# Weighted values of a block computed in two halves around one second-layer slice

## The chip, the cores and the metric

The kernel runs on one NeuronCore of a Trainium2 chip. The metric is the device time of one execution in microseconds (us), lower is better; the time before is the median of three runs. One further execution was taken with the hardware profiler, and every line shown below is of that execution. PE is TensorE (its weight loads are shown apart, as PEld), DVE is VectorE, ACT is ScalarE, POOL is GpSimd, SP is SyncE, which issues most DMAs.

## The reference

Attention with a banded mask and eight global keys, then a two-layer network on its output:

```python
scores = scale * np.matmul(q, k.transpose(0, 1, 3, 2)) + bias      # 4 batches, 8 heads, 768 rows, 64 columns
scores = np.where(keep, scores, -1e9)                               # the last 96 keys and the first 8
a = exp(scores - max); a = a / (sum(a) + 1e-9)
x = (a @ v)                                                         # 3072 rows of 512
h = x @ w_in                                                        # 512 -> 2048
out = (h * np.clip(h + 3.0, 0.0, 6.0) / 6.0) @ w_out                # 2048 -> 512
```

## The kernel before

The 3072 rows are worked on in 8 blocks of 384 rows (two for each batch, numbered 0 to 7). For each block the kernel makes the attention output x, then runs the two layers over 16 slices f of the 2048 hidden columns. `first` (L172) is the first layer of a slice: 12 matmuls of 128x384 into one PSUM bank named hp, of which there are two. `gate`, `high` and `rest` (ACT, DVE, POOL, DVE) turn hp into the pair gh and gl. `second` (L204) is the second layer of a slice: 9 matmuls of 128x512 into the three acc banks. The operands of both layers are in a float32 form that PE takes in one pass, so each such matmul leaves two PE records, one weight load and one matmul.

From block 2 on (`twos`, L490), slices go in twos: the first layer of two slices (L495), then `finish` of the two slices before (L500-501), and so on. Between these come `yield`s; at the k-th of them the caller runs the list `units[k]`, which holds the attention work of the next block (`attention`, L709). So while block i is in its layers, the attention of block i+1 is strewn between them. One round of `twos` has four yields, so k = 24 and 25 come after the first layers of slices 12 and 13, and k = 26 comes after the second layers of slices 10 and 11, just ahead of the first layers of slices 14 and 15.

Attention of a block, for each of four pairs of heads: `packed` makes the scores, then come softmax (DVE, ACT, POOL), a 32x32 transpose on DVE into the tile blocks (L948, `spread`) and four DMAs into the tile weights (`send`). The last pair's `send` is in units[21]. In units[26] stands `weighted` (L686): the products of weights with values for all four pairs. It walks over chunks of 32 keys, first the chunk of the global keys (384 wide) and then those of the band (32 to 128 wide). For each chunk it issues 8 matmuls, two for each pair, each on a 32x64 part of the PE array, and each pair adds up in a bank of its own: sp, tp, xp and one of the two hp banks. These operands are plain float32, which PE takes in two passes; each such matmul leaves four PE records. Blocks 3, 5 and 7 have 16 chunks (128 matmuls), blocks 4 and 6 have 13 (104 matmuls). After the last chunk `put_x` copies each bank to xh (ACT, L158) and xl (DVE, L159), which also frees the hp bank for slice 15, and a DMA fetches the next block's values (L309).

The order of PE, SP and POOL instructions is pinned to the program order (`in_order`, L663). DVE and ACT are ordered by a scheduler. Blocks 0 and 1 and the attention of block 2 (`rest_of_third`, L673) are worked on by other loops; `rest_of_third` calls `weighted` too.

## Time and profile before

| What | Value |
|---|---|
| median of 3 runs | 653.87 us (652.95 to 654.45) |
| the profiled execution | 655.53 us |
| its span, first to last instruction | 653.7 us |
| its mean granted PE clock | 0.995 of full speed |
| DVE, ACT, POOL busy | 54%, 39%, 25% of the span |
| HBM | 73 GB/s over the span |

The page gives busy time by engine, the chain of work that ended last, and groups of instructions. A timeline row has the start, the duration, engine, line, operation, the tile written and those read, the shape, a count, and in square brackets the idle time of the engine ahead of it with what ended it. "issue" there means that the engine waited for nothing that the profile shows. [...]

### The profile page before, as it was taken

How to read it: one execution, taken by the hardware profiler on the slowest of the kernel's cores; microseconds unless marked ns; L12 is line 12 of the kernel's file. 1: busy time of each engine (PE TensorE's matmuls, PEld its weight loads, DVE VectorE, ACT ScalarE, POOL GpSimd, SP SyncE). 2: the span in 40 equal slices, each digit the busy share in tenths (PEclk: the TensorE clock that was granted, in tenths of full speed). 3: DMA queues.
4: the chain of work that ended last, by engine and by line, in shares of the span. 5: the costliest groups of instructions: out<-in, count | busy, mean ns of one | idle time of the engine just before them, and what ended most of it. 6: DMA issues, size and time to landing. Idle time of an engine off the chain costs nothing.

```text
span 653.7 us, 14423 instructions
## 1 busy us (share of the span) xinstructions
PE 634.9 (97%) x5593; PEld 560.6 (86%) x5593; DVE 354.8 (54%) x1066; ACT 255.3 (39%) x706; POOL 166.5 (25%) x371
## 2 busy tenths in 40 slices
PE   8989999999999999999989999899999999999997
PEld 7778899888888888888978889888887888899985
DVE  5889999995645552356424554245523555222222
ACT  6897777775424321332223241143212522121111
POOL 5667000001423330134302332023310242012100
PEclk9999999999999999999989999899999999999999
DMA  7575454434423422233212241123311311110001
GB/s 281 181 239 173 138 159 156 141 120 142 117 60 116 117 59 44 81 108 81 67 67 77 59 117 31 67 78 82 93 31 66 102 38 31 33 40 10 1 1 54
DMA packets 34334, 59.78 MB, mean 91 GB/s; under 512 B 3280, under 2 KB 21200, under 8 KB 33488
## 3 DMA queue, kind: packets, MB, share of 16 engines
q1 hardware_dynamic: 33968, 58.50, 30.2%
q8 instruction: 46, 0.75, 0.5%
q14 instruction: 32, 0.26, 0.1%
q10 hardware_dynamic: 288, 0.26, 0.1%
HBM read 41.16 MB, written 6.29 MB: 73 GB/s over the span
## 4 chain that ended last, share of the span: by engine, by line
PE 88%; DVE 5%; ACT 2%; issue 2%; POOL 2%; DMA 1%; POOLq 0%; ACTq 0%
PE hp L172 40%; PE acc L204 35%; PE sp L873 2%; PE sp L204 2%; PE xp L204 1%; PE tp L204 1%; DVE xl L159 1%; ACT n L906 1%; POOL n L926 1%; PE sp L702 1%; DVE n L902 1%; PE tp L702 1%; PE xp L702 1%; DMA iv<-bounds 1%; PE tp L873 1%
## 5 line engine op out<-in xcount | busy, mean ns | idle before, releaser
L183 ACT ACTIVATE g<-hp,small 128x384 f32<-128x384 f32 x127 | 73.6, 580 | 264.3 <-PE hp L172 172.8
L172 PE MATMUL hp<-xh,w1h 128*128 128x384 f32 x512 | 175.2, 342 | 0.5 <-DVE xl L159 0.4
L172 PE MATMUL hp<-xh,w1l 128*128 128x384 f32 x512 | 173.9, 340 | 0.1
L172 PE MATMUL hp<-xl,w1h 128*128 128x384 f32 x512 | 173.1, 338 | 0.0
L190 POOL TENSOR_SCALAR gh<-g 128x384 fp32r<-128x384 f32 x104 | 53.3, 513 | 433.8 <-DVE g L184 405.0
L184 DVE SCALAR_TENSOR_TENSOR g<-g,hp 128x384 f32<-128x384 f32 x128 | 70.7, 553 | 125.4 <-ACT g L183 124.5
L204 PE MATMUL acc<-w2h,gh 128*128 128x512 f32 x336 | 132.7, 395 | 0.0
L204 PE MATMUL acc<-w2h,gl 128*128 128x512 f32 x336 | 131.8, 392 | 0.0
L204 PE MATMUL acc<-w2l,gh 128*128 128x512 f32 x336 | 131.7, 392 | 0.0
L197 DVE TENSOR_TENSOR gl<-g,gh 128x384 fp32r<-128x384 f32 x128 | 71.4, 558 | 66.1 <-POOL gh L190 60.3
L172 PEld LDWEIGHTS hp<-xh,w1h 128*128 128x128 f32 x512 | 97.3, 190 | 6.1 <-issue 1.9
L906 ACT ACTIVATE n<-n,least 128x136 f32<-128x136 f32 (+2 forms) x192 | 79.6, 416 | 53.6 <-DVE least L902 52.8
L172 PEld LDWEIGHTS hp<-xl,w1h 128*128 128x128 f32 x512 | 97.1, 190 | 2.6
L172 PEld LDWEIGHTS hp<-xh,w1l 128*128 128x128 f32 x512 | 97.0, 190 | 0.9 <-DVE w1l L439 0.8
L926 POOL TENSOR_SCALAR n<-n,sums 128x136 f32<-128x136 f32 (+2 forms) x186 | 81.8, 456 | 39.2 <-DVE sums L917 23.8
L204 PEld LDWEIGHTS acc<-w2h,gh 128*128 128x128 f32 x336 | 63.1, 188 | 14.7 <-issue 3.0
L204 PEld LDWEIGHTS acc<-w2h,gl 128*128 128x128 f32 x336 | 63.1, 188 | 13.7 <-DVE gl L197 0.3
L204 PEld LDWEIGHTS acc<-w2l,gh 128*128 128x128 f32 x336 | 63.1, 188 | 11.5
L948 DVE STREAM_TRANSPOSE blocks<-n 128x256 f32<-128x256 f32 x138 | 51.0, 423 | 22.6 <-POOL n L926 21.2
L906 ACT ACTIVATION_READ_ACCUMULATOR n<-n,least 128x1 f32 x192 | 36.0, 187 | 0.0
L399 ACT ACTIVATE wz<-wst 128x512 f32<-128x512 f32 x32 | 21.5, 676 | 5.9 <-DVE w2l L439 3.8
L446 DVE CUSTOM_DVE_ANT_0 wz<-wz,we 128x1024 uint16<-128x1024 uint16 x32 | 22.2, 695 | 1.2 <-POOL we L404 0.9
(126 smaller groups left out, 722.9 us busy)
## 6 DMA issues: line engine op xcount, KB each, us to landing
wst<-w SPq DMA_DIRECT2D x32, 512.0 KB, 3.6
load<-pairs SPq DMA_DIRECT2D x31, 444.0 KB, 3.5
weights<-blocks SPq DMA_DIRECT2D x92, 120.0 KB, 2.4
values<-values SPq DMA_DIRECT2D x6, 1024.0 KB, 5.0
out<-o SPq DMA_DIRECT2D x23, 256.0 KB, 2.3
values<-pairs SPq DMA_DIRECT2D x9, 384.0 KB, 3.4
out<-o ACTq DMA_DIRECT2D x1, 256.0 KB, 2.8
load<-pairs SPq DMA_DIRECT2D x1, 252.0 KB, 4.0
```

What stands on the lines that cost most here:

```text
L172: self.nc.tensor.matmul(hp, lhsT=self.w1(w, f)[:, kt, :], rhs=a[:, kt, :], start=(n == 0), stop=(n == 3 * NKT - 1))
L183: nc.scalar.activation(out=g, in_=hp, func=AF.Relu, bias=self.three, scale=1.0)
L184: nc.vector.scalar_tensor_tensor(out=g, in0=g, scalar=6.0, in1=hp, op0=ALU.min, op1=ALU.mult)
L190: self.nc.gpsimd.tensor_scalar(out=gh, in0=g, scalar1=1.0, scalar2=0.0, op0=ALU.mult, op1=ALU.add)
L197: self.nc.vector.tensor_tensor(out=gl, in0=g, in1=gh.bitcast(F32), op=ALU.subtract)
L204: self.nc.tensor.matmul(acc[tt], lhsT=a[:, tk], rhs=self.w2(w, f), start=(f == 0 and j == 0), stop=(f == NF - 1 and j == 2))
L399: self.nc.scalar.activation(out=self.z[i].bitcast(F32), in_=words[:, :, 1].bitcast(F32), func=AF.Abs)
L446: tt(out=z, in0=z, in1=self.e.pop(i), op=ALU.add)
L702: nc.tensor.matmul(out[pr][j * D:(j + 1) * D, g0 * GQ:g1 * GQ], lhsT=self.values_of[own, c, j * D:(j + 1) * D], rhs=groups[own, j, g0:g1, ...
L906: nc.scalar.activation(out=e[:, j, lo:end], in_=e[:, j, lo:end], func=AF.Exp, bias=self.least[:, i:i + 1], scale=-1.0, accum_out=self.sums ...
L926: nc.gpsimd.tensor_scalar(out=e[:, j, lo:end], in0=e[:, j, lo:end], scalar1=over, scalar2=0.0, op0=ALU.mult, op1=ALU.add)
L948: nc.vector.transpose(out=self.blocks[:, :, t, 4 * s:4 * s + 4], in_=e[:, :, c:c + P].rearrange("p j (b q) -> p j b q", b=4))
```

## The change

`weighted` becomes a generator that yields once, ahead of chunk number len(chunks) // 2. At k = 25 the caller puts its first half into a list, `between`; `twos` runs what is in that list after the second layer of the first of the two pending slices. The second half, with `put_x` and the DMA for the next values, stays at k = 26. For blocks 3 to 7 the order on PE is then: second layer of slice 10, first half of the products, second layer of slice 11, second half. The four banks hold partial sums over the second layer of slice 11. In `rest_of_third` the generator is run through at once, so the products of block 2 stay in one piece.

```diff
@@ twos
             for self.last in self.pending:
                 self.finish()
+                if self.between:
+                    self.between.pop()()
@@ banded
-        self.pending = []
+        self.pending, self.between = [], []
@@ rest_of_third
-        units[2 * slices - 1].append(lambda: self.weighted(pairs[:-1]))
+        units[2 * slices - 1].append(lambda: list(self.weighted(pairs[:-1])))
@@ weighted
-        for c, g0, g1, slot in chunks:
+        for n, (c, g0, g1, slot) in enumerate(chunks):
+            if n == len(chunks) // 2:
+                yield
@@ attention
-        units[26].append(lambda: self.weighted(pairs[:NPAIR]))
+        values = self.weighted(pairs[:NPAIR])
+        units[25].append(lambda: self.between.append(lambda: next(values)))
+        units[26].append(lambda: next(values, None))
```

PE's order before, for block 3: the last three matmuls of slice 11's second layer, then the products, whose chunk of the global keys (64x384 as the program counts the two halves of a row) comes first.

```order
L204 MATMUL acc<-w2h_1030,gh 128x512
L204 MATMUL acc<-w2l_1031,gh 128x512
L204 MATMUL acc<-w2h_1030,gl 128x512
L702 MATMUL sp<-weights,values 64x384 x2
L702 MATMUL tp<-weights,values 64x384 x2
L702 MATMUL xp<-weights,values 64x384 x2
L702 MATMUL hp<-weights,values 64x384 x2
L702 MATMUL sp<-weights,values 64x32 x2
```

All 64 rows of products follow one another there. Now the same place on PE with the change (L702 has become L706): what stands ahead of the eighth chunk's end and behind it.

```order
L706 MATMUL tp<-weights,values 64x128 x2
L706 MATMUL xp<-weights,values 64x128 x2
L706 MATMUL hp<-weights,values 64x128 x2
L204 MATMUL acc<-w2h_1030,gh 128x512
L204 MATMUL acc<-w2l_1031,gh 128x512
L204 MATMUL acc<-w2h_1030,gl 128x512
```

The nine L204 matmuls of slice 11, which stood ahead of the first product, now stand behind the 64th matmul of 128; the first half has moved nine matmuls forward, and the second half and everything after it stand where they stood. On DVE, ACT, POOL and SP nothing changes its order on the path that runs.

## The prediction

> **What bounds the kernel now.** The page first: how busy the engines are, the instruction queue, and who is on the chain that ended last.

> ```profile
> span 653.7 us, 14423 instructions
> PE 634.9 (97%) x5593; PEld 560.6 (86%) x5593; DVE 354.8 (54%) x1066; ACT 255.3 (39%) x706; POOL 166.5 (25%) x371
> ...
> q8 instruction: 46, 0.75, 0.5%
> ...
> PE 88%; DVE 5%; ACT 2%; issue 2%; POOL 2%; DMA 1%; POOLq 0%; ACTq 0%
> ...
> weights<-blocks SPq DMA_DIRECT2D x92, 120.0 KB, 2.4
> ```

> PE is the bound: 97% busy and 88% of the chain. A reorder on PE pays only if it removes time in which PE does nothing or runs slowly. Two per cent of the chain is "issue", so the second view is PE's timeline. These rows are, by time, the entry into block 3's products, the two rows around each stop inside the products of blocks 3 to 7, one row each of blocks 3 and 4 used below, and the rows where the first layer of slices 14 and 15 begins and where the second layer after it begins.

> ```profile
> 253.66 0.39 PE L204 MATMUL acc<-w2h,gl 128*128 128x512 f32 x1
> 253.98 0.54 PE L702 MATMUL sp<-weights,values 32*64 32x384 f32 x2
> ...
> 255.50 0.28 PE L702 MATMUL tp<-weights,values 32*64 32x128 f32 x2
> ...
> 257.25 0.24 PE L702 MATMUL sp<-weights,values 32*64 32x96 f32 x1
> 258.62 0.29 PE L702 MATMUL sp<-weights,values 32*64 32x96 f32 x1 [1.11 <-issue]
> ...
> 332.01 0.28 PE L702 MATMUL xp<-weights,values 32*64 32x128 f32 x2
> ...
> 333.73 0.24 PE L702 MATMUL xp<-weights,values 32*64 32x64 f32 x2
> 335.86 0.27 PE L702 MATMUL hp<-weights,values 32*64 32x64 f32 x2 [1.89 <-issue]
> ...
> 336.21 0.44 PE L172 MATMUL hp<-xh,w1h 128*128 128x384 f32 x1
> ...
> 342.04 0.39 PE L204 MATMUL acc<-w2h,gh 128*128 128x512 f32 x1
> ...
> 412.08 0.27 PE L702 MATMUL tp<-weights,values 32*64 32x96 f32 x2
> 414.10 0.30 PE L702 MATMUL xp<-weights,values 32*64 32x96 f32 x2 [1.76 <-issue]
> ...
> 414.77 0.45 PE L172 MATMUL hp<-xh,w1h 128*128 128x384 f32 x1
> ...
> 420.62 0.39 PE L204 MATMUL acc<-w2h,gh 128*128 128x512 f32 x1
> ...
> 490.41 0.22 PE L702 MATMUL hp<-weights,values 32*64 32x64 f32 x1
> 492.05 0.18 PE L702 MATMUL sp<-weights,values 32*64 32x32 f32 x1 [1.43 <-issue]
> ...
> 492.17 0.22 PE L702 MATMUL hp<-weights,values 32*64 32x32 f32 x2
> 492.32 0.44 PE L172 MATMUL hp<-xh,w1h 128*128 128x384 f32 x1
> 492.61 0.34 PE L172 MATMUL hp<-xl,w1h 128*128 128x384 f32 x1
> ...
> 497.07 0.39 PE L204 MATMUL acc<-w2h,gh 128*128 128x512 f32 x1
> ...
> 567.15 0.26 PE L702 MATMUL xp<-weights,values 32*64 32x96 f32 x2
> 568.61 0.30 PE L702 MATMUL hp<-weights,values 32*64 32x96 f32 x2 [1.19 <-issue]
> ```

> Each of the five blocks stops once inside its products, late, with no engine or data transfer named as the cause. From start to start the stops last 1.37, 2.13, 2.02, 1.64 and 1.46 us, 8.62 in all. Where do they come? The view of busy time by stretches, for L702 alone, counts the passes ahead of each stop (x behind the PE figure):

> ```profile
> 253.90:257.60 3.70, 3.53 (x211) 3.03 (x211) 1.00 0.01 4
> 330.60:334.20 3.60, 3.27 (x189) 2.87 (x190) 1.00 0.02 5
> 408.70:412.60 3.90, 3.61 (x216) 3.13 (x216) 1.00 0.02 4
> 487.30:490.90 3.60, 3.31 (x194) 2.90 (x195) 1.00 0.02 5
> 563.70:567.60 3.90, 3.66 (x221) 3.18 (x221) 1.00 0.01 4
> ```

> A pass is two records, so the stops come 422, 378, 432, 388 and 442 records into the products. A block's program has on PE 16 first layers of 24 records, 16 second layers of 18, four packed score groups of 96, and the products: 1568 records with 128 product matmuls, 1472 with 104. From stop to stop that makes 1568-422+378 = 1524, then 1526, 1524, 1526. The DMA view has the instruction queue's packets in between; these rows are the stretches from 256.2 to 333.6 us and from 333.5 to 333.6.

> ```profile
> q8 instruction: 6, 0.10, 0.5%
> ...
> q8 instruction: 1, 0.02, 59.1%
> ```

> Six packets between two stops (the three stretches after are alike), so one packet holds 1525/6 = 254 records. **Every stop is at a packet's edge, the second edge inside the same products.** My reading: PE's instructions arrive in packets, the next is fetched when an edge is passed, and it takes longer than PE needs for a packet of tiny matmuls. The edge before block 4's stop lies 127 passes earlier, at pass 62, about 332.0 us. From there the 127 passes run until 333.73, or 1.72 us; the packet moves at 333.5 and PE goes on at 335.86. So passing an edge to going on takes 3.85 us in the longest case (3.12 in block 3, by the same count from about 255.5).

> [...]

> A second loss follows the two longest stops. The view by stretches, now for all engines, from the first matmul after the products:

> ```profile
> 336.20:339.00 2.80, 2.80 (x14) 2.80 (x11) 1.95 (x4) 1.63 (x4) 0.00 (x0) 0.57 0.52 152
> 414.80:417.00 2.20, 2.20 (x11) 2.20 (x9) 1.76 (x4) 1.55 (x4) 0.00 (x0) 0.57 0.48 104
> ```

> The granted clock is 0.57 there. The two first layers take 342.04-336.21 = 5.83 and 420.62-414.77 = 5.85 us, against 497.07-492.32 = 4.75 in block 6, whose stop of 1.64 was followed by no dip. The dips cost 1.08 + 1.10 = 2.18 us.

> **The change part by part.** *Where the edges fall now.* The first half starts 18 records (one slice) earlier in the program, and what stands ahead of it is the same, so the edges keep their record numbers. The first edge falls 186, 142, 196, 152 and 206 records into the first half (stop minus 254 plus 18). That half holds 8 chunks or 256 records, 6 chunks or 192 in blocks 4 and 6. So in all five blocks the first edge is inside the first half, with 40 records to spare at least, and the second edge is inside the second half. The slice lies between them.

> *What the slice buys.* The chain of waits has 18 second-layer matmuls in one row:

> ```profile
> 559.71 4.12 PE acc L204 x18
> ```

> so nine take 2.06 us. Between the edges there are now 118 passes (1.60 us at 1.72 per 127), the slice (2.06) and one more change between array shapes each way (0.34, below): 4.00 us, where 1.72 stood. The longest need was 3.85. All five stops should end, by 0.15 us in block 4 and by more elsewhere: minus 8.62, plus 0.07 for five normal distances, is **minus 8.55**. A need 0.5 us longer than measured would leave some 0.35 in block 4, 0.3 in block 5, and nothing in block 3.

> *The dips.* Without the stops PE is idle for no stretch near 1.7 us there, and I take them as gone: **minus 2.18**. [...]

> *What is added.* One more way out of the products into full matmuls and one more way in, per block. Way in: 253.98-253.66 = 0.32 instead of 0.23 between starts, 0.09. Way out: from the last pass (492.17) to 492.32, and 0.29 instead of 0.17 to the next, together 0.25. That is 0.34 per block, **plus 1.7** for five. The trace has no way out to L204 in these blocks; the bounds are 0.09 a block (the weight loads hide) and 0.6 (twice the way out and the way in), 0.5 to 3.0 in all. I take 0.34, which is what both rows show.

> *What costs nothing, and why.* The first half starts 2.06 us earlier, in block 4 at 328.63 instead of 330.69. It needs the last weights: DVE's transposes and the bank of slice 12 are done early, as DVE's timeline has it:

> ```profile
> 321.81 0.77 DVE L948 STREAM_TRANSPOSE blocks<-n 128x256 f32<-128x256 f32 x2 [0.56 <-POOL n L926]
> ...
> 325.21 0.56 DVE L184 SCALAR_TENSOR_TENSOR g<-g,hp 128x384 f32<-128x384 f32 x1 [2.63 <-ACT g L183]
> ```

> The transposes end at 322.58 and the DMAs behind them land 2.4 us after issue by the page's median, so near 325, with 3.6 us to spare. The hp bank is free when slice 12's gate has read it, at 325.77, 2.9 us ahead. Gone cover would cost PE the lateness itself, once a block. Holding the banks costs nothing: sp, tp and xp are next asked for by the score groups of the next block, and the second hp bank by slice 15, after `put_x` as before. No DMA and no POOL or SP instruction moves. `put_x` stays behind the second half, so slice 15 waits for its bank as it does now; that is in the 4.75.

> Sum on the profiled execution: 655.53 - 8.55 - 2.18 + 1.7 = 646.5. That execution was 1.66 us over the median of the runs, about what one to two dips are worth, so the runs may hold fewer dips. Taking one from the median: 653.87 - 8.55 - 1.09 + 1.7 = **645.9**.

> **The rivals.** *The stop moves along (other side).* If the stop is set off by reaching the second edge at speed, not by time since the first, it keeps its length in the second half, and the change only adds 1.7: 655.6. It decides on when the fetch starts: at the first edge or at the end of what is there. Against it: in block 4 the packet moves at 333.5, before PE stops at 333.73. [...] 7%.

> *The fetch takes longer* than 4.0 us, because its start hangs on how far ahead PE reads and not on what PE executes: the longer stops keep up to 1 us each, and one dip may stay. About 649. For it: only 0.15 us to spare in block 4. 9%.

> *The dips stay*, from the low array use of the products: 653.87 - 8.55 + 1.7 = 647.0. Against it: blocks 3, 6 and 7 have the same products and no dip. 8%.

> *The split does nothing measurable*, savings and switches cancelling, near 653.5: 4%.

> **How the numbers follow.** The forecast holds 72%, with 643.5 (both dips in the runs, switches at 0.5) to 648.5 (switches at 3.0, small rests of the stops). The range 643.0 to 650.0 takes in the longer fetch and the staying dips and leaves out the other two, 11%, and some of the tails. A measurement of this kernel can tell about 0.2%, 1.3 us, from no change: faster 0.89, same 0.05, slower 0.06.

> **What would show it.** Right: no "issue" idle inside L706 in blocks 3 to 7, instruction packets still six to a block and the first edge in the first half, granted clock 1.0 in the first layers that follow, and L204 between two runs of L706 with starts of about 0.3 us at both joints. Wrong: an "issue" idle of over 1 us in a second half (the stop moves), the clock at 0.57 without one (the dips), joints far over 0.34 us, or PE waiting for DMA or DVE ahead of the first half.

## The result, and the profile after

The changed kernel takes 647.76 us (median of 4 runs, 647.15 to 648.35), against 654.16 (652.95 to 655.25, 4 runs): a ratio of 0.9903, 95% interval 0.9882 to 0.9923. The profiled execution took 647.65 us with a span of 645.9, against 655.53 and 653.7. The page of the changed kernel:

```profile
span 645.9 us, 14423 instructions
PE 634.3 (98%) x5593; PEld 557.5 (86%) x5593; DVE 354.9 (55%) x1066; ACT 255.9 (40%) x706; POOL 167.4 (26%) x371
```

The same instructions take 7.8 us less. PE's idle time fell by 7.2 us, from 18.8 to 11.6. Its busy time is hardly changed (634.9 us before, 634.3 now), because two things nearly cancel in it: the stretches of slow clock (2.25 us) went, and the joints (the changes between the products and full matmuls, 2.4 us, both below) came. The view of waits of PE (what waited, for what; us, times, longest) shows the idle time that is left:

```profile
PE xp L972 <- DVE xl L159: 1.9, 3, 1.1
PE xp L972 <- issue: 1.4, 1, 1.4
PE tp L940 <- ACT pt L944: 1.0, 1, 1.0
PE xp L386 <- DVE small L108: 0.9, 1, 0.9
PE sp L897 <- DMA load<-pairs: 0.6, 1, 0.6
PE hp L172 <- DVE xl L159: 0.3, 2, 0.2
```

No wait of L706, the products, is left in any of the five blocks, for "issue" or for a transfer. The 1.4 us of "issue" at L972 belongs to the first stage and stands in the trace before as well (1.42 us ahead of 44.26). PE's timeline around blocks 3 and 4 has the joints and the first layers that follow:

```profile
252.24 0.40 PE L204 MATMUL acc<-w2h,gl 128*128 128x512 f32 x1
252.57 0.54 PE L706 MATMUL sp<-weights,values 32*64 32x384 f32 x2
...
254.70 0.28 PE L706 MATMUL hp<-weights,values 32*64 32x128 f32 x2
254.91 0.50 PE L204 MATMUL acc<-w2h,gh 128*128 128x512 f32 x1
255.25 0.39 PE L204 MATMUL acc<-w2l,gh 128*128 128x512 f32 x1
...
256.86 0.39 PE L204 MATMUL acc<-w2h,gl 128*128 128x512 f32 x1
257.18 0.32 PE L706 MATMUL sp<-weights,values 32*64 32x128 f32 x2
...
326.19 0.39 PE L204 MATMUL acc<-w2h,gh 128*128 128x512 f32 x1
...
334.26 0.45 PE L172 MATMUL hp<-xh,w1h 128*128 128x384 f32 x1
...
338.97 0.39 PE L204 MATMUL acc<-w2h,gh 128*128 128x512 f32 x1
```

The second half follows the slice at the distance of the first entry, 0.32 us; the way out of the first half takes 0.21 and then 0.34 instead of 0.23. These are distances from start to start: the rows overlap, as L204 has a duration of 0.39 us where the next starts 0.23 later. Behind block 4 the two first layers take 338.97 - 334.26 = 4.71 us, where 5.83 stood, and the clock, in the view by stretches from 334.2 to 338.9 us, is full:

```profile
334.20:338.90 4.70, 4.54 (x36) 4.18 (x27) 2.85 (x6) 2.21 (x5) 0.51 (x1) 1.00 0.64 228
```

From the start of slice 10's second layer to the start of slice 14's first layer, blocks 3 to 7 are 0.92, 1.66, 1.62, 1.14 and 0.97 us shorter, 6.31 in all. The two dips give 2.25 more (1.12 and 1.13). What stands ahead of block 3, where nothing was changed, took 0.62 longer in this execution; the difference of the spans, 7.8, is these three to within 0.2.

### The profile page after: what moved, and what is told of

Same layout as the page of the kernel before. It is cut to its first block, busy times and chain, and to the rows that moved or that the text cites. A ratio compares the mean times of both kernels' runs of the same rounds, so it can differ in the third digit from the quotient of the medians.

```text
span 645.9 us, 14423 instructions
## 1 busy us (share of the span) xinstructions
PE 634.3 (98%) x5593; PEld 557.5 (86%) x5593; DVE 354.9 (55%) x1066; ACT 255.9 (40%) x706; POOL 167.4 (26%) x371
## 4 chain that ended last, share of the span: by engine, by line
PE 89%; DVE 4%; ACT 3%; DMA 1%; POOL 1%; issue 1%; SPq 0%; POOLq 0%; ACTq 0%; DVEq 0%
PE hp L172 40%; PE acc L204 36%; PE sp L879 2%; DVE xl L159 2%; PE sp L204 2%; PE tp L204 1%; PE xp L204 1%; PE sp L706 1%; ACT n L912 1%; DMA wst<-w 1%; POOL n L932 1%; PE tp L706 1%; DMA load<-pairs 1%; PE xp L972 1%; PE sp L897 1%
## 5 line engine op out<-in xcount | busy, mean ns | idle before, releaser
L183 ACT ACTIVATE g<-hp,small 128x384 f32<-128x384 f32 x127 | 73.8, 581 | 261.3 <-PE hp L172 174.5
L172 PE MATMUL hp<-xh,w1h 128*128 128x384 f32 x512 | 174.2, 340 | 0.7 <-DVE xl L159 0.3
L172 PE MATMUL hp<-xh,w1l 128*128 128x384 f32 x512 | 172.4, 337 | 0.1
L172 PE MATMUL hp<-xl,w1h 128*128 128x384 f32 x512 | 171.7, 335 | 0.0
L184 DVE SCALAR_TENSOR_TENSOR g<-g,hp 128x384 f32<-128x384 f32 x128 | 70.7, 552 | 122.0 <-ACT g L183 120.7
L204 PE MATMUL acc<-w2h,gh 128*128 128x512 f32 x336 | 133.2, 396 | 0.0
L204 PE MATMUL acc<-w2h,gl 128*128 128x512 f32 x336 | 131.9, 393 | 0.0
L204 PE MATMUL acc<-w2l,gh 128*128 128x512 f32 x336 | 131.7, 392 | 0.0
L172 PEld LDWEIGHTS hp<-xh,w1h 128*128 128x128 f32 x512 | 96.1, 188 | 7.0 <-DVE xl L159 2.3
L172 PEld LDWEIGHTS hp<-xl,w1h 128*128 128x128 f32 x512 | 96.1, 188 | 2.6
L172 PEld LDWEIGHTS hp<-xh,w1l 128*128 128x128 f32 x512 | 96.1, 188 | 0.9 <-DVE w1l L439 0.8
L204 PEld LDWEIGHTS acc<-w2h,gh 128*128 128x128 f32 x336 | 63.1, 188 | 15.4 <-issue 3.8
L204 PEld LDWEIGHTS acc<-w2h,gl 128*128 128x128 f32 x336 | 63.0, 188 | 13.8 <-DVE gl L197 0.3
L204 PEld LDWEIGHTS acc<-w2l,gh 128*128 128x128 f32 x336 | 63.1, 188 | 11.3
```

What stands on the lines that cost most here:

```text
L172: self.nc.tensor.matmul(hp, lhsT=self.w1(w, f)[:, kt, :], rhs=a[:, kt, :], start=(n == 0), stop=(n == 3 * NKT - 1))
L183: nc.scalar.activation(out=g, in_=hp, func=AF.Relu, bias=self.three, scale=1.0)
L184: nc.vector.scalar_tensor_tensor(out=g, in0=g, scalar=6.0, in1=hp, op0=ALU.min, op1=ALU.mult)
L204: self.nc.tensor.matmul(acc[tt], lhsT=a[:, tk], rhs=self.w2(w, f), start=(f == 0 and j == 0), stop=(f == NF - 1 and j == 2))
```

## The experiments

**Moving the edges and nothing else.** In the kernel before, the warm-up matmuls at its start become fewer and wider.

```diff
-        any_ = self.three.broadcast_to([P, P])
-        for _ in range(n):
-            self.nc.tensor.matmul(self.idle, lhsT=any_, rhs=any_, start=True, stop=True)
+        any_ = self.three.broadcast_to([P, P])
+        for m in [3] * (n // 3) + [n % 3] * (n % 3 > 0):
+            self.nc.tensor.matmul(self.idle[:, 0:m * P], lhsT=any_, rhs=self.three.broadcast_to([P, m * P]), start=True, stop=True)
```

> The kernel before, with the 29 warm-up matmuls of 128 columns at its start replaced by 11 of up to 384 columns: the same columns stream through PE, but 72 PE records fewer stand ahead of everything. Fetch theory (a stop comes where PE passes the second packet edge sooner than about 3.1 to 3.9 us after the first): every edge moves 72 records, 36 passes, later in the products. Blocks 3 and 5 stop at about passes 247 and 252 of 256, still 1.4 and 2.0 us; block 7's edge falls just behind its products, on the first matmuls of slice 14, about 1.3 us; in blocks 4 and 6 the edge falls 36 and 46 records behind the 208 passes, some 18 first-layer matmuls on, and there is no stop, and no clock dip behind block 4. Profiled time about 655.5 - 2.1 - 1.6 - 1.1 = 650.7. Burst theory (a run of tiny matmuls longer than about 190 passes drains something, wherever the edges are): the stops stay at passes 211, 189, 216, 194, 221, time about 655.

Measured: 649.64 us against 654.49, one run each. PE's timeline of this kernel, at the end of the products of blocks 3, 4, 5 and 7:

```profile
257.93 0.22 PE L702 MATMUL tp<-weights,values 32*64 32x32 f32 x1
259.45 0.24 PE L702 MATMUL tp<-weights,values 32*64 32x32 f32 x1 [1.30 <-issue]
...
326.48 0.39 PE L204 MATMUL acc<-w2h,gh 128*128 128x512 f32 x1
...
333.90 0.23 PE L702 MATMUL hp<-weights,values 32*64 32x32 f32 x2
334.06 0.44 PE L172 MATMUL hp<-xh,w1h 128*128 128x384 f32 x1
...
409.16 0.24 PE L702 MATMUL xp<-weights,values 32*64 32x32 f32 x2
410.91 0.30 PE L702 MATMUL hp<-weights,values 32*64 32x32 f32 x4 [1.51 <-issue]
...
562.37 0.44 PE L172 MATMUL hp<-xh,w1h 128*128 128x384 f32 x1
564.00 0.44 PE L172 MATMUL hp<-xl,w1h 128*128 128x384 f32 x1 [1.19 <-issue]
```

Blocks 3 and 5 stop after 247 and 252 passes, 36 later than before. Blocks 4 and 6 do not stop, with 208 passes in one piece. In block 7 the stop has left the products: it is at the second matmul of a first layer, an ordinary large one. The clearest view is a count from the program's start. The first three rows are of the kernel before and end inside the stops of blocks 3, 5 and 7; the other three are of this kernel and end inside its three stops (x behind the PE and PEld figures counts the records):

```profile
0.00:258.50 258.50, 251.10 (x2111) 220.18 (x2111) 190.81 (x558) 151.24 (x395) 74.81 (x169) 1.00 0.45 141
0.00:413.90 413.90, 402.81 (x3636) 354.51 (x3636) 261.16 (x790) 195.72 (x537) 115.28 (x257) 1.00 0.39 116
0.00:568.20 568.20, 554.53 (x5161) 488.85 (x5161) 331.86 (x1023) 240.18 (x679) 155.18 (x344) 0.99 0.35 102
```

```profile
0.00:259.20 259.20, 251.90 (x2111) 216.18 (x2111) 191.16 (x559) 151.64 (x396) 75.26 (x169) 1.00 0.47 141
0.00:410.50 410.50, 401.70 (x3636) 348.78 (x3636) 261.73 (x792) 196.87 (x540) 115.97 (x257) 1.00 0.40 117
0.00:563.50 563.50, 553.43 (x5161) 483.16 (x5161) 332.57 (x1025) 241.46 (x683) 156.11 (x344) 1.00 0.36 103
```

Both kernels stop after the same records, 4222, 7272 and 10322. An edit some 250 us earlier in the program, which changes no product, slides the products past these places by the 72 records that it removes. The burst theory falls here, since a full-sized matmul stops too and 208 passes run through.

**Splitting ahead of the first edge.** The changed kernel with another split point.

```diff
-            if n == len(chunks) // 2:
+            if n == 2:
```

> The changed kernel, but split after 2 chunks (32 passes) and not in the middle: the slice stands ahead of the first edge in all five blocks. Fetch theory: nothing stands between the edges, so all five stops come back at their old places in the program, 1.4 to 2.1 us each, 8.6 in all, with the dips of the clock behind the longest (0 to 2.2), and the extra joints stay: 647.7 + 8.6 + 0 to 2.2 = 656.3 to 658.5, no better than the kernel before. Burst theory: the second part has 224 or 176 passes, so the three longer blocks may stop near their end and blocks 4 and 6 not at all: 648 to 652.

Measured: 654.85 us. The rows of PE's timeline on which the five blocks go on again:

```profile
259.83 0.29 PE L706 MATMUL sp<-weights,values 32*64 32x96 f32 x1 [1.47 <-issue]
...
336.75 0.27 PE L706 MATMUL hp<-weights,values 32*64 32x64 f32 x2 [1.15 <-issue]
...
414.18 0.30 PE L706 MATMUL xp<-weights,values 32*64 32x96 f32 x2 [1.77 <-issue]
...
491.20 0.18 PE L706 MATMUL sp<-weights,values 32*64 32x32 f32 x1 [1.26 <-issue]
...
567.99 0.29 PE L706 MATMUL hp<-weights,values 32*64 32x96 f32 x2 [1.19 <-issue]
```

All five stops are back, after 211, 189, 216, 194 and 221 passes, which are exactly the places of the kernel before. From start to start they last 1.73, 1.38, 2.03, 1.48 and 1.46, 8.1 us. So the split alone takes no stop away here; in the changed kernel, where the stops are gone, the slice stands between the two edges. The time is 1.5 us below the expectation's lower end, which counts no dip. The stops were half a microsecond shorter in all (8.1 against 8.6); from slice 10 to slice 14 the five blocks are 7.5 us longer than in the changed kernel, so the shorter stops explain about half of what is missing from the 8.6, and the rest is open. No dip followed, although block 5's stop of 2.03 (row above, idle 1.77) was as long as the one that had a dip before.

**Splitting only blocks 3, 5 and 7.**

```diff
-            if n == len(chunks) // 2:
+            if n == (len(chunks) // 2 if tb else 0):
```

> The changed kernel with the split in blocks 3, 5 and 7 only; blocks 4 and 6 have their products in one piece again. Fetch theory: stops in blocks 4 and 6 alone, at passes 189 and 194, 2.1 and 1.6 us, a clock dip behind block 4 if its idle is 1.7 or more; two joints fewer (0.9): 647.7 + 3.8 - 0.9 + 0 to 1.1 = 650.6 to 651.7. If the products stopped for a reason that hangs on the whole program (its start, the transfers in flight), the other blocks would change too. Burst theory: the same two stops.

Measured: 648.74 us. PE's timeline has two stops in the products, in blocks 4 and 6:

```profile
332.75 0.24 PE L706 MATMUL xp<-weights,values 32*64 32x64 f32 x2
334.18 0.27 PE L706 MATMUL hp<-weights,values 32*64 32x64 f32 x2 [1.19 <-issue]
...
484.89 0.22 PE L706 MATMUL hp<-weights,values 32*64 32x64 f32 x1
486.32 0.18 PE L706 MATMUL sp<-weights,values 32*64 32x32 f32 x1 [1.21 <-issue]
```

The places are the expected ones (passes 189 and 194) and the other blocks are as in the changed kernel: each block's stop hangs on its own slice. The total is 1.9 us below the expectation's lower end. The lengths of the stops, 1.43 both, are below the 2.1 and 1.6 of the profile before, which is 0.9 of it; another 0.7 is the stage ahead of block 3, which this edit doesn't touch (slice 10's second layer of block 3 starts at 249.69 us here and at 250.39 in the changed kernel). How long the stop of one block lasts differs from run to run: 2.13, 1.38 and 1.43 in block 4.

**Less time between the edges.** Slice 11's second layer is cut: two thirds ahead of the first half, three matmuls between the halves.

```diff
-            for self.last in self.pending:
-                self.finish()
-                if self.between:
-                    self.between.pop()()
+            for n, self.last in enumerate(self.pending):
+                if n and self.between:
+                    self.second(*self.last[1:], (0, 1))
+                    self.between.pop()()
+                    self.second(*self.last[1:], (2,))
+                    self.last = None
+                else:
+                    self.finish()
```

> The changed kernel with only the last third of slice 11's second layer (3 matmuls, 0.7 us) between the halves; the other six stand ahead of the first half. Fetch theory: from edge to edge PE now needs 1.68 + 0.69 + 0.40 = 2.8 us against 3.1 to 3.9 that the fetch takes, so shortened stops remain: about 0.3, 1.1, 1.0, 0.6, 0.4 us in blocks 3 to 7, 3.4 in all, and no clock dips: 647.7 + 3.4 = 651.1. Burst theory, or any pause at all being enough: both halves are as short as in the changed kernel, no stops, 647.7.

Measured: 649.76 us. Around the old places of the stops in blocks 4, 6 and 7, PE's timeline now has

```profile
334.30 0.23 PE L710 MATMUL xp<-weights,values 32*64 32x64 f32 x2
334.60 0.27 PE L710 MATMUL hp<-weights,values 32*64 32x64 f32 x2
...
486.13 0.22 PE L710 MATMUL hp<-weights,values 32*64 32x64 f32 x1
486.50 0.18 PE L710 MATMUL sp<-weights,values 32*64 32x32 f32 x1 [0.15 <-issue]
...
562.09 0.26 PE L710 MATMUL xp<-weights,values 32*64 32x96 f32 x2
562.74 0.30 PE L710 MATMUL hp<-weights,values 32*64 32x96 f32 x2 [0.40 <-issue]
```

Rests of 0.30, 0.37 and 0.65 us from start to start, at the same places (blocks 3 and 5 have rests of 0.24 and 0.22). Against the changed kernel the five blocks are 0.33, 0.28, 0.34, 0.33 and 0.67 longer, 1.95 in all, where 3.4 was expected: the right kind of answer at a smaller size. If the three matmuls take the 1.05 us off each stop that the expectation counts (2.8 less 1.72), the whole stops of that run would have been some 1.3 to 1.7 us, about as long as in the two runs before this one, and not up to 2.1. "Any pause is enough" falls: it would have left nothing.

**Three parts, for the price of the joints.**

```diff
-            if n == len(chunks) // 2:
+            if n in (len(chunks) // 3, 2 * len(chunks) // 3):
-        units[25].append(lambda: self.between.append(lambda: next(values)))
+        units[25] += [lambda: next(values), lambda: self.between.append(lambda: next(values))]
```

> The changed kernel with the products in three parts: one ahead of slice 10's second layer, one between slices 10 and 11, one behind. No stop can come back by the fetch theory (the first edge falls into the second part, the second into the third, with a slice between), so the run shows one more pair of joints per block by itself. From the halves against the unsplit products without a stop (8.07 against 7.58 us in block 4) a pair costs 0.48: 647.7 + 2.4 = 650.1, and each block's section from slice 10 to slice 14 0.48 longer plus the part that moved. If the first part came too early for its weights, PE would wait for a transfer there.

Measured: 653.32 us, 3.2 more than expected and within the runs of the kernel before (652.44 to 655.56), though no stop is left. The waits of PE, PE's timeline in block 5, and SP's row with the four DMAs of block 5's last weights:

```profile
PE sp L706 <- PE hp L172: 2.0, 4, 0.5
...
PE sp L706 <- DMA weights<-blocks: 0.4, 1, 0.4
```

```profile
403.55 0.34 PE L172 MATMUL hp<-xh,w1l 128*128 128x384 f32 x1
404.37 0.54 PE L706 MATMUL sp<-weights,values 32*64 32x384 f32 x2 [0.48 <-PE hp L172]
```

```profile
399.86 2.55 SPq L960 DMA_DIRECT2D weights<-blocks  x4
```

A block takes about 1.2 us more than in the changed kernel, not 0.48. The first product starts 0.82 us after the last matmul of the layer ahead of it, where the distance behind a second layer was 0.33 (252.24 to 252.57). The row names PE's first layer as the releaser, but that had ended at 403.89, 0.48 us earlier. What came last is the weights: the last of the four DMAs is issued at 401.80, and with the 2.4 us that they take to land it is there at 404.2, just ahead of the first product at 404.37. In all five blocks the first product starts 2.5 to 2.6 us after that last issue, and in block 7, whose wait names the DMA, the landing is recorded 0.13 us ahead of it. So in this kernel every block waits 0.4 to 0.5 us for its weights. With the 0.48 for the joints, 0.2 to 0.3 of the 1.2 us stays open. The run failed as a clean price of a joint, and shows how early the products can be let in before their weights are late.

**Splitting only where an edge asks for it.** The changed kernel with the fewer warm-up records of the first experiment and

```diff
-            if n == len(chunks) // 2:
+            if n == (12 if tb else 0):
```

> The changed kernel with the 72 records fewer at the start, no split in blocks 4 and 6 (the second edge now falls some 36 and 46 records behind their products), and the split of blocks 3, 5 and 7 after 12 of 16 chunks, since their first edge now falls some 258, 268 and 278 records in. Fetch theory: no stop anywhere in the products and two pairs of joints fewer, 0.96: 647.8 - 1.0 = 646.8. Burst theory: 208 passes in one piece stop again in blocks 4 and 6 and 192 in the others, 650 or more.

> The changed kernel once more, beside the one that splits only where needed, on the same chip: 647.2 to 648.4 as before, no stops, and against the kernel before 0.990, where single runs of the latter differ by the number of clock dips (granted clock 0.995 with two, 0.999 with none).

Measured on one chip: 647.04 us (646.51 to 647.87, 6 runs) for the new one, ratio to the kernel before 0.9905 (0.9889 to 0.9922), and 647.33 (646.84 to 648.07) for the changed kernel, ratio 0.9910 (0.9893 to 0.9927). The two can't be told apart. Block 4 in PE's timeline of the new one:

```profile
325.87 0.39 PE L204 MATMUL acc<-w2h,gh 128*128 128x512 f32 x1
...
333.46 0.44 PE L172 MATMUL hp<-xh,w1h 128*128 128x384 f32 x1
```

and of the changed kernel again:

```profile
325.62 0.39 PE L204 MATMUL acc<-w2h,gh 128*128 128x512 f32 x1
...
333.71 0.45 PE L172 MATMUL hp<-xh,w1h 128*128 128x384 f32 x1
```

That is 7.59 against 8.09 us; the 0.5 is the price of one pair of joints without a stop in either. Blocks 4 and 6 save 0.5 each, blocks 3, 5 and 7 lose 0.06, 0.26 and 0.06. No stop is left in any block. My count for this kernel had missed an edge: with one 258 to 278 records in, there is another 254 earlier, 4 to 24 records into the products, and no slice between those two. In block 5 the packet nearest that edge moves within the first 0.1 us of the products, and in blocks 3 and 7 it moves 0.2 and 0.5 us ahead of them, where in the changed kernel the first packet of a block moves 2.3 to 2.6 us in. That is 2.3 to 3.0 us earlier against the products, and block 5's 0.26 us are all that shows of the two edges without a slice between them. The count had not foreseen that, and how much time was to spare was not measured.

## Why the prediction came out as it did

*PE is the bound, and the loss is in its stops.* Right: PE's instructions are the same before and after, and the idle time at the products is gone.

*Every stop is at the second packet edge of the products.* Shown by the first experiment, in which the stops keep their record numbers while the products move, and by the second, which brings them back with the split in place. The row of before that decided for it was the packet count, six between two stops.

*The slice between the edges outlasts the fetch, 4.00 us against 3.85.* Right in all five blocks, in both profiles of the changed kernel. By the count of records PE takes 4.1 to 4.2 us from edge to edge in the changed kernel, and in all traces that have stops in the products it took 3.1 to 3.9 from passing the first edge to going on (3.16, 3.87, 3.82, 3.35 and 3.22 in the trace of before). The experiment with three matmuls between shows that the margin was real and not wide: with 2.8 us, rests of 0.2 to 0.7 stay. One part of the reading was too simple, that the fetch starts when PE passes an edge. Inside the products of the kernel before and of the changed one the packet moves 0.7 to 1.6 us after the edge. In the layers ahead of block 3 it moves before it: in the trace of before at 224.42 and 241.03 us, where PE comes to the next edge, by the same count, at 228.6 and 245.4. So the packet does not wait for the edge in every stretch. That its start goes with how far PE has read ahead, the ground of a rival in the prediction, would fit, but no trace shows how far that is and no run tried it.

*The dips go.* In the two profiles of the changed kernel none of the five blocks has one. But the reason, the length of a stop alone, was too simple. Idle times of 1.89 and 1.76 us (before) and 1.51 (first experiment, block 5) were followed by a dip; 1.77 and 1.47 (second experiment, blocks 5 and 3) were not. The clock of before has a pattern that could fit all of them. It is 0.50 from 336.60 to 340.01 and from 415.10 to 418.51 us, 3.413 us each time, and falls once more at 654.03, 0.3 us behind the last instruction. From one fall to the next are 78.51 and 238.93 us, or 23 and 70 times 3.413. If a count in steps of that length is kept, the three idle times with a dip each lie whole inside the step that ends where the dip begins (333.18 to 336.60 and 411.69 to 415.10 in the trace of before). In the second experiment the clock falls only at the end, at 651.63; 70 steps earlier, at 412.70, a step would end in the middle of block 5's idle time (412.41 to 414.18) and cut it into 0.28 and 1.48. Counted so, the stops with a dip had 1.51 to 1.89 us of idle time in one step, and no stop in the products with 1.48 or less was followed by one. That the clock is set by such steps, and that they lie differently against the stops from run to run, is an estimate from these times, made afterwards; no run tried it.

*The joints.* This term was too small: 0.34 a block in the prediction, 0.48 to 0.50 by the pairs with and without a split (8.07 against 334.06 - 326.48 = 7.58 for block 4 in the first experiment, 8.09 against 7.59 in the last), 2.4 in all instead of 1.7. The two rows that I had were the right ones, way in and way out, but the way out to a second layer costs 0.05 more than that to a first layer, and some 0.1 is in neither row.

*From the profiled execution to the median.* Here the forecast lost most of its 1.9 us. By the prediction's own sum the profiled execution would take 646.5; it took 647.65, of which 0.7 are the joints and 0.6 the stage ahead of block 3, which differs that much between runs. For the median I counted one dip among the runs of before. Of 11 later runs of that kernel the median is 652.99, and seven of them have a mean clock of 0.998 or more (the profiled one 0.995, with two dips; the traces without a dip 0.998 to 1.0). So the usual run has no dip to lose. Without that term the sum was 647.0, and with the joints at their measured 2.4 it is 647.7. That this is the measured time to within 0.1 us is partly luck: the stops add up to 8.6 us in the profile of before and to 8.1 in the second experiment, and the median of the kernel before was 653.87, 654.16 and 652.99 in three sets of runs.

*What costs nothing.* Right for the changed kernel: there is no wait of the first half for weights or banks. But the 3.6 us to spare were misread. They hold for the first of four DMAs, and SP issues the four one after another, as its row in the trace of before has it:

```profile
322.61 2.57 SPq L954 DMA_DIRECT2D weights<-blocks  x4
```

The last is issued at 324.56 and, with the page's median of 2.4 us, lands at 326.96, which leaves 1.7 us ahead of 328.63. With three parts the first starts 2.06 us earlier still, and there every block waits for its weights.

*The rivals.* The stop that moves along was the wrong mechanism: no stop is left in a second half. The second experiment shows its price, though: with the slice outside the edges the kernel takes 654.85 us (one run without a dip), 1.9 over the 652.99 of the kernel before on another chip and 0.4 over the one run beside it. Both are within the joints' 2.4. A fetch longer than the slice and dips that stay are in neither profile of the changed kernel, and a split without effect is excluded by the interval, 0.9882 to 0.9923. From block 3 on, PE is idle for no more than 0.19 us ahead of any full-sized matmul of the two layers in the traces of before and of the changed kernel; the first experiment has 1.19 us in block 7 (row above).

## What to carry to other kernels

An idle stretch of the bound engine with no releaser named, at odd places in a run of very short instructions, is worth counting: number its instructions, compare with the instruction queue's packets, and see whether the stops lie a whole number of packets apart. Not every such stretch goes with a packet: PE's 1.4 us of "issue" in the first stage lasts 1.42 us before and 1.43 in the changed kernel at the same matmul, though in the changed kernel a packet moves from 43.16 to 44.09 us, into the idle time (43.49 to 44.92), and in the trace of before none moves from 31.0 to 46.4 us. Where the stops did lie so, in this kernel, they went when a slice of 2.06 us came between two edges and not when the burst was only made shorter (five stops, 8.1 us, in the second experiment), and 72 records fewer at the start of the program moved them. Price the joints by a pair of runs with and without them, and don't take from a median what only some of its runs have.

## What was not expected of the hardware

The stops hang on record numbers and not on what stands there (4222, 7272 and 10322 with the products shifted by 72): 72 records fewer at the start brought 649.64 us by themselves, 4.85 less than the kernel before beside it (one run each), against 6.4 for the change. In the trace of before the instruction packet begins to move 2.3 to 2.9 us before PE goes on; by its row in the prediction (59.1% of 16 engines in 0.1 us) it takes about 0.95 us of one DMA engine (0.88 to 1.47 in the five blocks), so most of the time behind its start is not the moving of its 16 KB (46 packets, 0.75 MB on the page). And where an edge lies within the first records of the products, the packet can move ahead of them: by 0.2 and 0.5 us in blocks 3 and 7 of the kernel that splits only where needed, and within 0.1 us of their start in block 5.
